# Transposed weights read in contiguous blocks, a narrow split on VectorE, one load queue and a new step order

## The chip, the cores and the metric

The kernel runs on one core of a Trainium2 chip. The metric is the device time of one execution in microseconds (us), the median of repeated runs. The core's engines work side by side: PE (TensorE) multiplies matrices; DVE (VectorE), ACT (ScalarE) and POOL (GpSimd) work on elements; SP (SyncE) issues DMAs here, as ACT can too.

## The reference, cut to what matters

```python
def phi(x):                                  # attention, 4 batches, 4 heads, 1088 tokens, head_dim 32
    a = np.einsum('rd,bhsd->bhsr', S1, x)    # S1, S2: 8 x 32
    b = np.einsum('rd,bhsd->bhsr', S2, x)
    return np.einsum('bhsi,bhsj->bhsij', a, b).reshape(*x.shape[:-1], r * r)
q_p, k_p = (phi(q), phi(k))
kv = np.einsum('bhsf,bhsd->bhfd', k_p, v)
z = np.sum(k_p, axis=2)
num = np.einsum('bhsf,bhfd->bhsd', q_p, kv)
den = np.einsum('bhsf,bhf->bhs', q_p, z)[..., None] + 1e-06
x = num / den                                # then regrouped to 4352 x 128
a = x @ w1                                   # 128 x 1024
b = x @ w2
h = a * b @ w3                               # 1024 x 1024
out = h @ w_out                              # 1024 x 128
```

q, k and v are float32. S1, S2 and the four weights are float64 and arrive as raw 64-bit words.

## The kernel before, in words

**Weights.** The 64-bit words of w1, w2, w_out and w3 come in eleven pieces of 1 MB, `w0` to `w10`: `w0` and `w1` are halves of w1 and w2, `w2` is w_out (called wo), `w3` to `w10` are the eight 128-row blocks of w3. A piece lands in a buffer `raw` (three of them) and is turned into float32 by five steps: `.c` (scaled high words), `.s` (the sign) and `.m` (rounding bits from the low words), three passes on ACT (L337, L345, L349); `.j` on DVE (L360) joins exponent and mantissa; `.a` (L365) adds the sign and rounding words, on POOL for `w3` to `w6` and on DVE for the others. `.load` brings the piece on SP's queue; for w3 it brings two of four 32-row quarters, and `.load2` brings the other two on ACT's queue.

**Fold.** Since the second product follows directly on the first, the kernel computes w3o = w3 @ w_out once. For block ko, step `f{ko}.t` (L392) transposes the block in 32x32 tiles on DVE, `f{ko}.m` (L398) multiplies it with wo in eight steps, and `f{ko}.o` copies the result into w3o.

**Attention.** For each batch b the steps `k{b}.*` load k and v, split k, form the gram matrix of k (`gram`), its pieces `G*`, `T*` and `N*`, the k features `kp` and their product with v (`kv`, `kvr`), from which `kz` or `ky` are made. `kr0` and `kr1` take the last 64 tokens of two batches. `s.*` prepare S1 and S2: `s.words` and `s.pair` turn their words into float32, `s.split` splits each into a leading part and a rest, on POOL, writing every value four times over for the heads, and `s.lead` (ACT) copies the leading part likewise; `s.T` transposes them and `s.P` multiplies them.

**Groups.** The tokens go in eight groups of 512, g = 0 to 7, and a rest of 256, r. The steps `q{g}.*` make the features of the queries (`A0`, `C0`, `sm` and the rest up to `phi`) and multiply them with kz or ky (`x`), up to the group's input `xT`. For group 0 the last steps are `x` and `xt` on PE, `xs` on DVE, `xT` on ACT. Then for each of eight column blocks c of w1 and w2: `g{g}.{c}a` and `g{g}.{c}b` multiply (L1179, L1189), `.c` copies the first product out of PSUM (ACT, L1184), `.m` multiplies the two into `ab` (DVE, L1195), and `g{g}.{c}o` (L1203) adds ab times w3o to the group's output. The output is transposed by `oT` and stored by `st`. PSUM tag "h" has three buffers, shared by a, b, the folds and some small products.

**What sets the order.** `make_steps` returns a dictionary of steps, and the constant `ORDER` names all of them in one list. They are issued in that order, and each engine works on its own instructions in that order: an instruction that waits holds all later ones of its engine. SP's loads have a further rule: with `DEPTH = 4`, a DMA on SP waits until the fourth one before it has landed. The steps `warm0` to `warm9` issue matmuls on zeros (L183) that compute nothing, as many as `WARM` says. `POOL` names the steps that go to GpSimd instead of VectorE.

Of the kernel before, what the change touches and what calls it, by code (L numbers as in the profile page):

```python
# [11 lines left out]
F32 = mybir.dt.float32  # L12
BF16 = mybir.dt.bfloat16
F16 = mybir.dt.float16
I32 = mybir.dt.int32
# [10 lines left out]
WARM = [10, 2, 1, 1, 1, 1, 3, 3, 3, 2]  # L26

BY_PE = ()
QUEUE2 = "act"

DEPTH = 4
# [3 lines left out]
POOL = set("s.split k1.rest k2.rest k1.kp0 k1.kp1 k2.kp0 k2.kp1 w3.a w4.a w5.a w6.a".split())  # L35
# [3 lines left out]
c.zeros k0.zero k0.load0 k0.loadr c.mask k0.load1 s.load c.act s.zero q0.load c.ident w0.load k0.max0 k0.max1  # L39
k0.nat1 w1.load k0.nat0 warm0 k0.tr1 k0.g0 k0.g1 k0.lead0 s.words k0.lead1 k0.l160 k0.rest0 k0.l161 warm1  # L40
k0.gram0 k0.rest1 k0.kT1 s.pair k0.gram1 q0.tr s.split s.lead q0.max w0.c warm2 s.T k0.Gm k0.Gt k0.Ga k0.Gr
q0.l2 k1.zero k1.loadr k1.load kr0.load k0.Gb s.P q0.l1 s.blk s.Pp warm3 k0.ab1 k0.tr0 k0.abc1 w2.load s.blkh
w1.c q0.rm k0.T0 k0.T1 k0.kp1a kh1.load q0.A0 k0.Ta warm4 q0.C0 k0.kT0 k1.max w1.s k0.kp1b k0.Tb w0.m k1.g
q0.sma warm5 k0.N0 k1.lead k0.Ts q1.tr k1.l16 k1.rest warm6 k0.N1 k0.ab0 k0.Na q0.sta kr0.tr k1.gram0 k0.Nb
kr0.kT w1.m q1.max k0.Nh k0.Nl w0.j q0.A1 k0.abc0 k1.gram1 k0.Nf w0.s q0.sha k0.kp0a q0.smy q0.sla kr0.ab k1.kT0
q0.C1 w2.c q0.sca k0.kp0b k1.kT1 q0.C1t q1.l2 q0.sty q0.al q0.shy kr0.abc q1.l1 q0.phi kr0.kp v0.zero v0.load
v0.loadr w3.load kr1.load warm7 k0.kv0 k0.kv1 k0.kv3 k1.gram2 w3.load2 k0.kv2 k2.zero k2.loadr k0.kvr q0.sly
q0.pt0 k0.kvm q0.scy w4.load q0.p01 q0.pt1 q0.pc0 q0.p2 k0.kzt w0.a k1.ab q0.pc1 k2.load k0.kz w4.load2 q0.x
q0.p12 k1.abt w2.m q0.dn k1.Gm q0.de q0.rc w2.s q0.xs w5.load w1.j warm8 q0.xt q1.A0 w2.j q0.xT k1.Gt w5.load2
w1.a warm9 g0.0a w3.c g0.0b q1.sm w2.a g0.1a g0.0c w3.s g0.0m g0.2a k1.Gr g0.1b g0.1c q1.rm g0.2c g0.2b w3.m  # L50
g0.1m w3.j kr1.tr g0.6a w4.c g0.2m w6.load w3.a g0.5a q1.st k2.max g0.6c g0.6b w6.load2 g0.3a k0.kw kr1.kT
q0.restT g0.5c k2.g k2.lead q1.C0 w4.s g0.6m k2.rest f0.t g0.3c g0.5b w4.m k1.Ga q1.sh g0.3b w5.c w7.load w4.j
f0.m k1.Gb q1.load w4.a k2.l16 g0.5m q1.sl w5.m g0.4a g0.3m q1.sca k2.gram0 q1.scy q1.p01 w5.s q1.al k2.gram1
q1.p2 w5.j k2.gram2 f0.o g0.4c q1.p12 k1.T0 k1.T1 w5.a g0.4b f1.t w7.load2 g0.7a w6.c q1.dn k1.Ta g0.0o g0.4m
k1.kp0 w6.m f1.m f2.t w6.s k2.Gm k1.Tb v1.zero v1.loadr w8.load v1.load k3.zero w6.j f2.m g0.7c q1.de q1.restT
f1.o w6.a q2.tr q1.rc q2.max g0.1o f2.o w7.m q1.bs k0.kyt k1.kp1 f3.t g0.2o k3.loadr w8.load2 k3.load g0.7b
q3.tr w10.load w7.c kr1.ab q1.phi f3.m kr1.abc w7.s w9.load w7.j q1.pt1 f3.o w7.a w10.load2 q1.pt0 k1.kv0 q1.pc0
k1.kv3 f4.t k1.kv2 q1.pc1 k1.kv1 k1.kvr g0.3o k0.ky w8.c k2.Gt g0.7m kh2.load f4.m k2.Gr w8.m k1.kw q3.max
k3.max q1.x f4.o g0.4o q1.xT k3.g w8.j w8.s k3.lead g1.1a k1.Ts g1.2a k3.rest q2.l2 g1.1c g1.1b g1.2c w8.a
k3.l16 k1.N0 g1.2b g1.1m w9.load2 k1.N1 g1.4a g1.2m f5.t g1.7a g1.4c w10.c g1.4b k1.Na k1.Nb g1.7b g1.7c k2.Ga  # L60
g1.4m q2.l1 f5.m w10.m w10.j k1.Nl g1.7m w10.s k1.Nh q2.rm k1.kyt g1.0a f5.o g1.5a w10.a w9.c g0.5o k1.ky k2.Gb
w9.s k2.kT1 g1.5b k1.Nf k2.kT0 q2.C0 g1.0c w9.j kh3.load w9.m f7.t k2.ab g1.5c q3.l2 q2.A0 k3.gram0 k2.abt
# [41 lines left out]
def make_steps(ctx, tc, q, k, v, S1, S2, moe_w1, moe_w2, moe_w3, moe_w_out, out):  # L104
# [136 lines left out]
    def _():  # L241
# [7 lines left out]
        for i in range(2):  # L249
            dve.tensor_scalar(t[:, i], hi[:, i], m[:, i:i + 1], m[:, i:i + 1], ALU.add, ALU.subtract)  # L250
# [1041 lines left out]
```

## Time and profile before

| what | us |
|---|---|
| median of 3 runs | 273.92 (271.85 to 274.69) |
| the profiled execution | 269.56 |
| its span, from the first to the last instruction | 267.8 |
| PE busy | 255.1 (95%) |
| VectorE busy | 189.2 (71%) |
| ACT busy | 112.1 (42%) |
| POOL busy | 35.6 (13%) |
| moved by DMA | 22.52 MB, mean 84 GB/s |

The profile is of one execution, so its times are compared with its own span, not with the median. A group of instructions is shown with its source line, the engine, what it writes and reads, shapes, count, busy us and mean ns, and then the engine's idle time before it with what ended it. The rows of digits cut the span into 40 slices of 6.7 us, each digit the busy share in tenths. Matmuls are pipelined: the busy time of PE includes waits inside the pipeline. A float32 matmul shows as two records.

### The profile page before, as it was taken

The page shows a single profiled execution, that of the slowest core. Times are in us where ns is not written, and L with a number is a line of the kernel's source. Part 1 is how long each engine was busy: PE and PEld are TensorE (multiplying, and loading weights), DVE is VectorE, ACT ScalarE, POOL GpSimd, SP SyncE. Part 2 cuts the span into 40 slices and gives each one's busy share as a digit, 9 for nine tenths or more (in the row PEclk, how much of TensorE's full clock was granted, in tenths as well). Part 3 has the DMA queues.
Part 4 walks back from the last instruction along what each step waited for, and adds up shares of the span by engine and source line. Part 5 has one row for each costly group of instructions (what it writes and reads, how often), then busy time and mean ns, then how long its engine had stood idle before and what let it go on. Part 6 is the DMA issues. An engine that isn't in the chain of part 4 may idle for free.

```text
span 267.8 us, 5767 instructions
## 1 busy us (share of the span) xinstructions
PE 255.1 (95%) x2336; PEld 142.0 (53%) x2336; DVE 189.2 (71%) x430; ACT 112.1 (42%) x192; POOL 35.6 (13%) x55
## 2 busy tenths in 40 slices
PE   7789999799898999999999999999999999999994
PEld 2567745476545685444545444444544444444484
DVE  4878899998999999968948959775474645134141
ACT  5486688966689600323322323333113221232220
POOL 3436106675000440000000000000000000000000
PEclk9986999999999999999999999999999999999999
DMA  6888799988970503504100200020020002002020
GB/s 202 281 268 204 159 223 211 230 214 203 219 169 5 163 5 52 157 0 104 21 4 0 40 2 0 2 42 0 2 40 0 2 0 39 0 2 39 0 39 20
DMA packets 31226, 22.52 MB, mean 84 GB/s; under 512 B 21344, under 2 KB 25568, under 8 KB 31072
## 3 DMA queue, kind: packets, MB, share of 16 engines
q1 hardware_dynamic: 28352, 17.44, 27.5%
q10 hardware_dynamic: 2848, 4.72, 7.4%
q8 instruction: 18, 0.29, 0.5%
q14 instruction: 8, 0.07, 0.1%
HBM read 19.93 MB, written 2.23 MB: 83 GB/s over the span
## 4 chain that ended last, share of the span: by engine, by line
PE 69%; DVE 13%; DMA 10%; ACT 4%; issue 1%; POOL 1%; SPq 0%; DVEq 0%; ACTq 0%
PE ps_o L1203 19%; PE b_ps L1189 19%; PE a_ps L1179 19%; DMA raw<-in_moe_w_dram 5%; DVE w3T L392 5%; DMA kk<-in_k_dram 4%; PE ps_xb L1123 3%; PE ps_c L859 2%; PE ps_w3o L398 2%; DVE ab L1195 2%; PE ps_o L1207 1%; DMA s_raw<-in_S_dram 1%; DVE k_g L147 1%; DVE w3c L365 1%; POOL w3c L365 1%
## 5 line engine op out<-in xcount | busy, mean ns | idle before, releaser
L1195 DVE TENSOR_TENSOR ab<-ffa,b_ps 128x512 f32<-128x512 f32 (+1 forms) x72 | 46.6, 650 | 55.7 <-PE b_ps L1189 40.9
L1184 ACT COPY ffa<-a_ps 128x512 f32<-128x512 f32 (+1 forms) x72 | 40.2, 564 | 98.4 <-PE a_ps L1179 89.8
L1189 PE MATMUL b_ps<-xT,w 128*128 128x512 f32 (+1 forms) x144 | 69.2, 574 | 0.0
L1179 PE MATMUL a_ps<-xT,w 128*128 128x512 f32 (+1 forms) x144 | 68.2, 572 | 0.1
L1203 PE MATMUL ps_o<-ab,w3o 128*128 128x512 f32 x128 | 64.3, 600 | 0.0
L1179 PEld LDWEIGHTS a_ps<-xT,w 128*128 128x128 f32 x144 | 26.4, 190 | 29.3 <-issue 23.7
L1189 PEld LDWEIGHTS b_ps<-xT,w 128*128 128x128 f32 x144 | 26.5, 190 | 28.0 <-issue 24.7
L1203 PEld LDWEIGHTS ps_o<-ab,w3o 128*128 128x128 f32 x128 | 23.1, 190 | 25.3 <-issue 21.4
L398 PE MATMUL ps_w3o<-wo,w3T 128*128 128x128 f32 x128 | 15.7, 278 | 3.8 <-DVE ab L1195 2.5
L398 PEld LDWEIGHTS ps_w3o<-wo,w3T 128*128 128x128 f32 x128 | 14.9, 192 | 7.4 <-DVE ab L1195 4.5
L392 DVE STREAM_TRANSPOSE w3T<-w3c 128x1024 f32<-128x1024 f32 x8 | 16.6, 2075 | 0.9 <-POOL w3c L365 0.8
L349 ACT ACTIVATE sg<-raw 128x1024 uint16<-128x1024 uint32 x11 | 15.1, 1377 | 0.8 <-DVE s_pr L1031 0.8
L345 ACT CAST sg<-cv_c 128x1024 f16<-128x1024 f32 x11 | 15.2, 1380 | 0.0
L337 ACT ACTIVATE cv_c<-raw 128x1024 f32<-128x1024 f32 x11 | 12.8, 1161 | 2.7 <-DMA raw<-in_moe_w_dram 1.6
L1137 ACT COPY xT<-ps_xb 128x128 f32<-128x128 f32 (+1 forms) x28 | 5.7, 281 | 16.8 <-PE ps_xb L1123 16.8
L536 POOL TENSOR_TENSOR kp<-kabt 128x1024 f32<-128x1024 f32 x4 | 8.6, 2160 | 27.1 <-DVE kabt L595 27.0
L365 POOL TENSOR_TENSOR w3c<-w3c,sg 128x1024 int32<-128x1024 int32 x4 | 9.6, 2406 | 17.1 <-DVE w3c L360 14.1
L183 PE MATMUL idle_ps<-zeros 128*128 128x512 bf16 x27 | 10.0, 491 | 1.1 <-DVE zeros L158 1.1
L1058 DVE TENSOR_TENSOR ph<-s_al,s_bs 128x1024 f32<-128x1024 f32 (+1 forms) x8 | 9.2, 1144 | 0.1
L836 ACT ACTIVATE q<-qT,q_m 128x512 f32<-128x512 f32 x8 | 5.8, 726 | 6.8 <-DVE s_rc L1045 3.5
L513 PE MATMUL ps_g<-kk 128*32 128x64 f32 x288 | 8.4, 235 | 0.1
L147 DVE TENSOR_REDUCE k_g<-kk 128x1 f32<-128x1152 f32 (+1 forms) x5 | 5.5, 1107 | 4.3 <-DMA kk<-in_k_dram 4.3
(215 smaller groups left out, 312.0 us busy)
## 6 DMA issues: line engine op xcount, KB each, us to landing
raw<-in_moe_w_dram SPq DMA_DIRECT2D x16, 256.0 KB, 5.8
raw<-in_moe_w_dram ACTq DMA_DIRECT2D x16, 256.0 KB, 6.2
qh<-in_q_dram SPq DMA_DIRECT2D x4, 544.0 KB, 4.0
raw<-in_moe_w_dram SPq DMA_DIRECT2D x4, 512.0 KB, 8.0
out_dram<-oT SPq DMA_DIRECT2D x32, 64.0 KB, 2.0
kk<-in_k_dram SPq DMA_DIRECT2D x3, 512.0 KB, 6.8
kh<-in_k_dram SPq DMA_DIRECT2D x12, 128.0 KB, 4.5
v<-in_v_dram SPq DMA_DIRECT2D x12, 128.0 KB, 3.3
```

Source lines behind the costliest of these rows:

```text
L183: pe.matmul(t, zeros[:, :128], bview(zeros, [[0, 2], [1, 256]]), start=True, stop=True)
L337: act.mul(x["c"], words(1).bitcast(F32), 2.0 ** -112)
L345: act.copy(sign, x["c"])
L349: act.mul(bview(sign_bits[n % 2].bitcast(U16), [[2, 1024]]), words(0).bitcast(U32), 2.0 ** -29)
L365: on(f"w{n}.a").tensor_tensor(d, d, sign_bits[n % 2], ALU.add)
L392: dve.transpose(w3T[ko].rearrange("p s (i r) -> p s i r", r=32), bview(w3c[ko], [[1, NC], [256, 4], [NC, 32]]))
L398: pe.matmul(t["o"], w3T[ko][:, c], wo[:, c], start=c == 0, stop=c == NC - 1)
L1179: pe.matmul(x["a"][:, :w], w_of(0, c), xT[g][:, c0:c0 + w], start=True, stop=True)
L1184: act.copy(x["s"][:, :w], x["a"][:, :w])
L1189: pe.matmul(x["b"][:, :w], w_of(1, c), xT[g][:, c0:c0 + w], start=True, stop=True)
L1195: dve.tensor_mul(ab_sb[g, c][:, c0:c0 + w], x["s"][:, :w], x["b"][:, :w])
L1203: pe.matmul(o_ps[g][:, :n], w3o[:, c], ab[:, :n], start=c == 0, stop=c == NC - 1)
```

## The change

1. A w3 block is transposed from contiguous runs of 32 elements: column 32s + r of a quarter, where it was 8r + s. To match, wo is loaded by 32-row quarters too, so that partition p of slice s holds row 256(p // 32) + 32s + p % 32. It gets a `.load2` of its own.
2. `s.split` goes from POOL to DVE and writes each value once; `s.lead` then makes all four parts for the heads in one copy, and `s.P` reads the narrow values.
3. `.load2` goes from ACT's queue to SP's (`QUEUE2`), and `DEPTH` from 4 to 6.
4. `w3.s` and `w5.s` go from ACT to POOL.
5. `ORDER` is new throughout, and so are the places and the number of the idle matmuls: 41 in six places for 27 in ten.

The helper `shape` in the diff leaves every access as it was, since `BY_PE` is empty.

```diff
-WARM = [10, 2, 1, 1, 1, 1, 3, 3, 3, 2]
+WARM = [14, 3, 5, 14, 2, 3]
-QUEUE2 = "act"
+QUEUE2 = "sp"
-DEPTH = 4
+DEPTH = 6
-POOL = set("s.split k1.rest k2.rest k1.kp0 k1.kp1 k2.kp0 k2.kp1 w3.a w4.a w5.a w6.a".split())
+POOL = set("k1.rest k2.rest k1.kp0 k1.kp1 k2.kp0 k2.kp1 w3.a w4.a w5.a w6.a w3.s w5.s".split())
 ORDER = """
-c.zeros k0.zero k0.load0 k0.loadr c.mask k0.load1 s.load c.act s.zero q0.load c.ident w0.load k0.max0 k0.max1
-k0.nat1 w1.load k0.nat0 warm0 k0.tr1 k0.g0 k0.g1 k0.lead0 s.words k0.lead1 k0.l160 k0.rest0 k0.l161 warm1
-k0.gram0 k0.rest1 k0.kT1 s.pair k0.gram1 q0.tr s.split s.lead q0.max w0.c warm2 s.T k0.Gm k0.Gt k0.Ga k0.Gr
-q0.l2 k1.zero k1.loadr k1.load kr0.load k0.Gb s.P q0.l1 s.blk s.Pp warm3 k0.ab1 k0.tr0 k0.abc1 w2.load s.blkh
-w1.c q0.rm k0.T0 k0.T1 k0.kp1a kh1.load q0.A0 k0.Ta warm4 q0.C0 k0.kT0 k1.max w1.s k0.kp1b k0.Tb w0.m k1.g
-q0.sma warm5 k0.N0 k1.lead k0.Ts q1.tr k1.l16 k1.rest warm6 k0.N1 k0.ab0 k0.Na q0.sta kr0.tr k1.gram0 k0.Nb
-kr0.kT w1.m q1.max k0.Nh k0.Nl w0.j q0.A1 k0.abc0 k1.gram1 k0.Nf w0.s q0.sha k0.kp0a q0.smy q0.sla kr0.ab k1.kT0
-q0.C1 w2.c q0.sca k0.kp0b k1.kT1 q0.C1t q1.l2 q0.sty q0.al q0.shy kr0.abc q1.l1 q0.phi kr0.kp v0.zero v0.load
-v0.loadr w3.load kr1.load warm7 k0.kv0 k0.kv1 k0.kv3 k1.gram2 w3.load2 k0.kv2 k2.zero k2.loadr k0.kvr q0.sly
-q0.pt0 k0.kvm q0.scy w4.load q0.p01 q0.pt1 q0.pc0 q0.p2 k0.kzt w0.a k1.ab q0.pc1 k2.load k0.kz w4.load2 q0.x
-q0.p12 k1.abt w2.m q0.dn k1.Gm q0.de q0.rc w2.s q0.xs w5.load w1.j warm8 q0.xt q1.A0 w2.j q0.xT k1.Gt w5.load2
-w1.a warm9 g0.0a w3.c g0.0b q1.sm w2.a g0.1a g0.0c w3.s g0.0m g0.2a k1.Gr g0.1b g0.1c q1.rm g0.2c g0.2b w3.m
-g0.1m w3.j kr1.tr g0.6a w4.c g0.2m w6.load w3.a g0.5a q1.st k2.max g0.6c g0.6b w6.load2 g0.3a k0.kw kr1.kT
-q0.restT g0.5c k2.g k2.lead q1.C0 w4.s g0.6m k2.rest f0.t g0.3c g0.5b w4.m k1.Ga q1.sh g0.3b w5.c w7.load w4.j
-f0.m k1.Gb q1.load w4.a k2.l16 g0.5m q1.sl w5.m g0.4a g0.3m q1.sca k2.gram0 q1.scy q1.p01 w5.s q1.al k2.gram1
-q1.p2 w5.j k2.gram2 f0.o g0.4c q1.p12 k1.T0 k1.T1 w5.a g0.4b f1.t w7.load2 g0.7a w6.c q1.dn k1.Ta g0.0o g0.4m
...
+c.zeros s.zero c.mask k0.zero k0.load0 k0.loadr k0.load1 s.load c.act q0.load v0.zero c.ident kr0.load k0.max0
+w0.load k0.max1 s.words v0.load k0.nat1 k0.g0 s.pair k0.nat0 k0.g1 k0.lead0 k0.lead1 k0.l160 k0.rest0 k0.l161
+warm0 k0.gram0 k0.rest1 s.split k0.gram1 q0.tr s.lead s.P k0.tr0 k1.zero k1.load k0.Gm q0.max k1.loadr s.T
+k0.kT0 q1.tr k0.tr1 kh1.load q0.l2 s.blkh k0.Gt s.blk q0.l1 k0.Ga k0.Gr warm1 k0.ab0 k0.kT1 q0.rm w1.load kr0.tr
+k0.ab1 k0.Gb k0.abc0 s.Pp k0.kp0a k0.abc1 kr0.kT w0.c k0.kp1a v0.loadr q1.max warm2 k0.T0 k0.T1 k0.kv0 w3.load
+q0.A0 k0.Ta k0.kp1b q0.C0 k1.max w3.load2 k0.kp0b k0.Tb kr0.ab q0.sma k0.kv1 k0.Ts k1.g k0.N0 q0.sta k1.lead
+k0.kv2 k0.kv3 k0.N1 q0.sha k1.l16 k1.rest k1.kT0 k0.Na w0.m q0.sla q0.sca k1.kT1 w1.m w2.load k0.Nb k0.Nh k0.Nf
+q0.al warm3 q0.A1 k0.Nl q0.C1 w2.load2 q0.smy kr0.abc w0.s q0.phi kr0.kp k1.gram0 k0.kvr q0.sty q1.l2 warm4
+q0.pt0 k0.kvm q0.shy q0.C1t q0.pt1 q0.sly q0.pc0 w0.j k0.kzt k1.ab q0.pc1 q0.scy k0.kz q0.p01 w1.c q0.x q0.p2
+k1.abt q1.l1 q0.p12 w5.load q0.dn w1.s q0.de q0.rc w5.load2 k1.gram1 q0.xs q1.A0 kr1.load w0.a q0.xt q0.xT w1.j
+w3.c warm5 g0.0a q1.rm g0.0b w2.c w1.a k1.gram2 g0.0c w3.j w3.s g0.3a w3.m k1.Gm k1.Gt q1.sm g0.7a g0.0m g0.3c
+w4.load w3.a g0.3b g0.7c g0.5a w5.c g0.3m q0.restT g0.7b k0.kw g0.5c q1.st w5.s f0.t w5.m g0.5b kr1.tr g0.2a
+q1.sh w2.m w5.j q1.C0 w2.j w5.a w2.s g0.7m q1.sl g0.5m g0.1a g0.2c q1.scy q1.sca g0.1b w2.a g0.1c k2.zero
+k2.loadr w4.load2 w7.load k2.load w7.load2 w6.load g0.2b w4.c g0.1m g0.6a kr1.kT w4.s q1.al w4.j f0.m w6.load2
+q1.p01 w4.m q1.p2 g0.2m q1.p12 g0.4a f2.t g0.6c w4.a q1.load g0.6b g0.4c k2.max f0.o k0.kyt g0.0o k0.ky q1.dn
+w7.c k2.g f2.m q1.de k2.lead g0.6m w7.m k2.rest f1.t g0.4b k2.l16 kr1.ab q1.rc k1.Ga f1.m q1.bs w7.s k1.Gr k1.Gb
...
     @step("s.split")
     def _():
         hi, lo = (x.rearrange("p (i d) -> p i d", i=2) for x in (sk["a"].bitcast(F32), sk["m"]))
-        m, t = sk["g"], sb("sk_t", [r, 2, D])
-        sk["abs"] = x = sb("pT", [r, 3, 2, H, D], name="sk_abs")
-        wide = lambda y: bview(y, [[D, 2], [0, H], [1, D]])
-        dve = on("s.split")
+        m, t = bview(sk["g"], [[1, 2], [0, D]]), sb("sk_t", [r, 2, D])
+        sk["x"] = x = sb("sk_x", [r, 6, D])
+        both = lambda n, by: bview(x[:, n], [[by * D, 2], [1, D]])
         dve.tensor_mul(sk["m"], sk["m"], sk["c"])
-        dve.tensor_scalar(m, m, 2.0 ** 16, None, ALU.mult)
-        for i in range(2):
-            dve.tensor_scalar(t[:, i], hi[:, i], m[:, i:i + 1], m[:, i:i + 1], ALU.add, ALU.subtract)
-        dve.tensor_add(x[:, 2], wide(hi), wide(lo))
-        dve.tensor_sub(hi, hi, t)
-        dve.tensor_add(x[:, 1], wide(hi), wide(lo))
-        sk["t"] = wide(t)
+        shift_in(dve, t, hi, m, 8)
+        shift_out(dve, both(0, 4), t, m, 8)
+        dve.tensor_sub(t, hi, both(0, 4))
+        dve.tensor_add(both(1, 2), hi, lo)
+        dve.tensor_add(both(2, 3), t, lo)
     @step("s.lead")
     def _():
-        act.copy(sk["abs"][:, 0], sk["t"])
+        sk["rep"] = sb("pT", [r, 4, H, D], name="sk_rep")
+        act.copy(sk["rep"], bview(sk["x"], [[D, 4], [0, H], [1, D]]))
...
-            elif n == 2:
-                sp.dma_start(raw[n], moe_w_out.rearrange("(p s) d -> p (s d)", s=NC))
             else:
                 quarter(sp, 0)
-                quarter(sp, 1)
+                quarter(sp, 2)
         def quarter(eng, t):
-            src = bass.AP(tensor=moe_w3.tensor, offset=moe_w3.offset + (n - 3) * 128 * DF + t * 256,
-                          ap=[[DF, 32], [32 * DF, 4], [1, 256]])
+            if n == 2:
+                src = bass.AP(tensor=moe_w_out.tensor, offset=moe_w_out.offset + t * 256 * DM,
+                              ap=[[DM, 32], [32 * DM, NC], [1, DM]])
+            else:
+                src = bass.AP(tensor=moe_w3.tensor, offset=moe_w3.offset + (n - 3) * 128 * DF + t * 256,
+                              ap=[[DF, 32], [32 * DF, 4], [1, 256]])
             eng.dma_start(raw[n][t * 32:(t + 1) * 32], src)
-        if n > 2 and n - 3 not in BY_PE:
+        if n >= 2 and n - 3 not in BY_PE:
             @step(f"w{n}.load2")
             def _():
-                for t in (2, 3):
+                for t in (1, 3):
                     quarter({"pool": pool, "act": act, "sp": sp}[QUEUE2], t)
...
             @step(f"f{ko}.t")
             def _():
                 w3T[ko] = sb("w3T", [128, NC, 128], bufs=2)
-                dve.transpose(w3T[ko].rearrange("p s (i r) -> p s i r", r=32), bview(w3c[ko], [[1, NC], [256, 4], [NC, 32]]))
+                dve.transpose(w3T[ko].rearrange("p s (i r) -> p s i r", r=32), bview(w3c[ko], [[32, NC], [256, 4], [1, 32]]))
```

The two beginnings of `ORDER` reach past the first FFN steps and the first fold; the later part is reordered likewise.

## The prediction, made before the changed kernel was run

> **What bounds the kernel now.** I read the slices of the span first, then the stages, then the chain of waits, then single stretches of the timeline.
>
> ```profile
> PE   7789999799898999999999999999999999999994
> DVE  4878899998999999968948959775474645134141
> PEclk9986999999999999999999999999999999999999
> DMA  6888799988970503504100200020020002002020
> ```
>
> PE is full from about the 15th slice (100 us) on; before that VectorE is as full as PE, and the DMA engines are near full for eleven slices. The same in four stages, cut at the first FFN matmul (`g0.0a`, 35.5) and at the end of `k3.gram2` (98.5); after the times stand busy us of PE, weight loads, DVE, ACT and POOL:
>
> ```profile
> 0.00:35.50 35.50, 30.47 (x449) 21.05 (x449) 26.71 (x80) 23.09 (x34) 13.47 (x41) 0.90 0.80 223
> 35.50:98.50 63.00, 59.03 (x677) 38.45 (x677) 60.42 (x112) 45.43 (x60) 22.10 (x14) 1.00 0.74 167
> 98.50:255.00 156.50, 156.39 (x1158) 74.45 (x1156) 99.07 (x234) 41.47 (x92) 0.00 (x0) 1.00 0.12 24
> ```
>
> PE's busy time counts waits inside the pipeline, so I price PE by the distance from start to start where it runs dense. In the chain, late:
>
> ```profile
> 119.37 0.86 PE a_ps L1179 x2
> ```
>
> An FFN step costs 0.86. So 192 steps make 165.0, the last group 10.4, eight folds of 1.89 make 15.1, and the q, k and S work, priced alike, 47.6: 238.1 us useful, plus 27 idle (warming) matmuls. Before `g0.0a` lie 17.6 us of it, so 220.5 remain, and 267.8 - 35.5 - 220.5 = 11.8 us are lost later: 5.0 in the second stage (58.0 of 63.0 used), 3.4 in small pieces after 98.5, 3.5 behind the last matmul. Only the start of `g0.0a` and those 5.0 us can move.
>
> What causes the 5.0: the view of L398, the folds' matmuls, gives who ended its idle time (us, times):
>
> ```profile
>   DVE ab L1195: 7.0, 5
>   DVE w3T L392: 3.4, 4
> ```
>
> Both enders are VectorE's (60.4 busy of 63). Its dearest item there is the w3 transpose, and the same operation on as many elements, read contiguously, takes 1.23 for 2.08; in the groups:
>
> ```profile
> L392 DVE STREAM_TRANSPOSE w3T<-w3c 128x1024 f32<-128x1024 f32 x8 | 16.6, 2075 | 0.9 <-POOL w3c L365 0.8
> L1069 DVE STREAM_TRANSPOSE pT<-ph 128x1024 f32<-128x1024 f32 x6 | 7.4, 1232 | 0.0
> ```
>
> What sets 35.5: in VectorE's timeline the start of `xs` follows a wait for `ps_kv` and a queue of other work, `w0.a` (L365) among it:
>
> ```profile
> 29.42 0.29 DVE L627 TENSOR_TENSOR kvm<-ps_kv,mask 128x128 f32<-128x128 f32 x1 [0.77 <-PE ps_kv L620]
> 30.37 1.22 DVE L365 CUSTOM_DVE_ANT_0 w<-w,sg 128x2048 uint16<-128x2048 uint16 x1
> 33.45 0.69 DVE L1101 TENSOR_TENSOR xs<-ps_xt,s_rc 128x512 f32<-128x512 f32 x1 [0.25 <-PE ps_xt L1095]
> ```
>
> In PE's timeline, what made `ps_kv` late, and three idle matmuls:
>
> ```profile
> 29.04 0.32 PE L620 MATMUL ps_kv<-kpr,v 128*32 128x64 f32 x8 [0.43 <-POOL v L443]
> 19.29 1.49 PE L183 MATMUL idle_ps<-zeros 128*128 128x512 bf16 x3
> ```
>
> `k0.kvr` waits for a POOL memset standing behind `kr0.kp`, and the phi transposes queue behind it. VectorE has done 25.2 us of work (start to start) when `xs` begins at 33.45; of the other 8.2, half is the wait for the first load, half is scattered waits like the one shown.
>
> [...] the granted clock was 0.50 in 20 to 24 us, and the three idle matmuls above took 0.43 each, against 0.21 warm. [...]
>
> **The change, part by part.**
>
> *Transposes.* The durations give 2.075 - 1.232 = 0.84, so 8 x 0.84 = 6.7 us off VectorE, all between 45 and 95 us. Bounds: 0, if the stride is not the cause, and 6.7; I take 6.7. It is worth only what PE waits for, at most the 5.0.
>
> *wo in 32-row quarters.* Four DMAs of 1 KB pieces for one of 8 KB pieces; k's loads have 1 KB pieces too, 512 KB in 6.8 us beside others. It is needed only by `f0.m` (45 us); nothing on the path.
>
> *S split.* POOL took 3.4 (8.53 to 11.94). Six small DVE operations at about 0.2 (the `s.pair` rows) are 1.2 on the full engine; `s.lead` grows from 0.40 to 0.59 (512 elements, ffa's row). Net VectorE: -6.7 + 1.2 = -5.5.
>
> *Signs w3.s, w5.s.* ACT loses 2 x 1.24. POOL has no such row: lower bound 1.1 (its 512-element product), upper 2.4 (L365); [...] I take 2.0. `w3.a` then waits on `w3.m` anyway (35.3), so both bounds cost nothing; if ACT did `w3.m` earlier, up to 2.4 on `f0.t`.
>
> *Queues.* 16 issues leave ACT (0.3 to 0.5 each, mostly under running operations: ACT idled only 0.35 us for issue), so I book nothing; at most 16 x 0.4 = 6.4 of ACT's time where ACT is late. SP gets 19 more, 119 in all at about 0.5: 60 us, and it has gaps. Six loads in flight for four. `k1.load` still waits for the grams (one kk buffer), about 10.6 for 12.1, and lands by 16; `k1.max`, which waited 1.15 us for it, is now due at 17.5. `w1.load`, issued at 5.2 before, now stands behind it: about 14.5, and is due at 22.8 (`w1.m`).
>
> *Waits added.* On ACT `k1.l16` waits for `k1.lead` (16.7 to 20.5), and behind it stands `w0.m`, which frees the buffer that `w2.load` needs on SP: 22.8; wo is due at 44. Behind `w2.load` stand `w5.load` (free after `w1.c`, 28.6; due 36) and `kr1.load` (due 39). `w4.load` waits for `w3.m` (35.3), `w7.load` for `w2.m` (40.3), and behind it stands `k2.load`: issued 41.5, and at 6.8 (kk's row) landed 48.3. If it is late, `k2.max` holds all of VectorE.
>
> *Idle matmuls.* 41 for 27: 14 more, 3.0 us at 0.21, 6.0 at 0.43. Fourteen cover the first loads; fourteen (`warm3`) stand in front of `q0.A1`, where VectorE's `k0.Nh` is due at 23.5 anyway: nothing if warm (20.6 + 3.0 = 23.6), up to 3 if cold. I take warm, since PE is busier there than before.
>
> *New order, walked by hand on all queues with these rows.* S words 5.5, `k0.rest1` 8.4, S split 9.6, grams 10.5 (10.0 before), `s.T` 12.1, `s.blk` 12.8, `k0.T1` 16.8 (15.0: five idle matmuls and `s.Pp` ahead), `k0.N1` 20.6 (21.0), `warm3` to 23.6, `k0.Nh` 23.5, `q0.smy` 24.0, phi 24.3 to 25.4 (28.4 before: `w0.j`, `q1.max` and `k1.kT` no longer stand between). `v0.zero` is early, so `kvr` ends 25.3; transposes 26.7; ACT copies and kz 27.5; `q0.x` 29.7; `xs` 30.4 (`w0.a` now behind it); `xT` 31.5; `g0.0a` 31.7. VectorE would be idle about 1 us in all after the first load, against about 4 before; [...] I take 32.7. 17.0 us useful precede it, so 221.1 remain.
>
> Then PE, walked to `f3.m` with three "h" buffers, never waits: f0 at 44.9, f2 49.7, f1 52.8, f4 59.2, f3 69.8. VectorE needs 49 us where PE needs 56 to `k3.gram2`, so the stage turns from VectorE's to PE's. Near misses: `k2.load` lands 48.3, `k2.max` is due 48.2; w4 and w7 land within 1 us of need. For them and jitter I leave 1.7 of the 5.0. The late 6.9 stay: 99.1 of 156.5 busy leaves VectorE slack there.
>
> Sum: 32.7 + 221.1 + 1.7 + 6.9 = 262.4, that is 5.4 under 267.8. The profiled execution took 269.56 (span + 1.8); the median, 273.92, lies 4.4 higher. I take the difference off the median: 268.5.
>
> **Rivals.**
>
> *The walk literally (265.8).* `g0.0a` at 31.7 and no loss in the second stage: 2.7 more gained. For: the walk. Against: the kernel before loses such pieces too.
>
> *Half the gain (272).* `warm3` runs cold: 14 x 0.43 = 6.0, or 4.7 if the clock returns midway, so `q0.A1` is 2 us late; and the folds wait for jitter as before (3.3 of 5.0 lost): 268.5 + 2.0 + 1.6 = 272.1. For: 0.50 at exactly that place. The change not doing what it says ends here too: if contiguous runs did not help the transpose, VectorE stays full, the 5.0 stay, and 271.8 results.
>
> *Slower: the single load queue (278).* From 35.3 (w3's buffer free) to w10, SP must bring 9.1 MB (six w3 blocks of 1.05, k2, q1, k3, v1, kh2). At 220 GB/s, about what full slices show, w10 lands at 76.7; `f7.m` is due about 86 and the conversion takes 6.5, so 79.5 is free. Each later us delays PE by one. At 170 GB/s it lands at 88.8: +9.3, 277.8. It decides against the change below 174 GB/s (landing 87.6). For: buffer waits block everything behind them, and 58 to 62 us, half idle, gives 138. Against: six in flight, and stages of 4 us between 30 and 58 show 191 to 265.
>
> **How the numbers follow.** Likeliest 0.46 (own range 266.5 to 270.5), literal walk 0.14, half 0.26, slower 0.14. About 1% (2.7 us) is what measurement tells apart. Faster: 0.46 + 0.14 + 0.08 of "half" = 0.68; same: 0.18 + 0.02 = 0.20; slower 0.12. The range reaches over the literal walk and "half" to 264.5 and 274.5; most of the slower case is left out.
>
> **What would show it.** Right: L392's successor near 1.23; `g0.0a` between 32 and 34; idle before the fold's matmuls below 3; phi ending by 27. Wrong: clock 0.5 around 20 to 25 with `warm3` over 4; `k2.max` or `w10`'s conversion waiting for DMA; `g0.0a` later than 34.5; PE idle for VectorE after 98 us.

## The result and the profile after

| | before | after |
|---|---|---|
| median of the runs side by side (four each), us | 272.88 (270.83 to 274.69) | 262.07 (261.84 to 262.68) |
| ratio | | 0.9609, 95% interval 0.9531 to 0.9688 |
| profiled execution, us | 269.56 | 261.84 |
| its span, us | 267.8 | 260.1 |
| its mean granted clock | 0.987 | 1.0 |
| first FFN matmul (`g0.0a`), us | 35.5 | 32.2 |
| end of the last fold's matmuls, us | 96.6 | 91.9 |

The kernel is faster by 3.9%. The forecast was 268.5, range 264.5 to 274.5: the sign is right, the size is 6.4 us short. Here and below, medians are of all runs, while ratios leave out those over 1.5% above the fastest of the same kernel.

The slices of the kernel after, in the same form as those of before:

```profile
PE   6899999999999999999999999999999999999994
DVE  3889979999999999879338958955889623232331
PEclk9999999999999999999999999999999999999999
DMA  6879979969899010260002002000200002020020
```

PE is now full from the third slice on instead of the 15th. The clock never falls. VectorE is still full in the middle, but PE no longer waits for it. The stages, cut at `g0.0a` and at the end of the last gram (columns as before):

```profile
0.00:32.23 32.23, 28.78 (x427) 19.85 (x427) 25.60 (x82) 19.83 (x32) 9.99 (x33) 1.00 0.88 232
32.23:88.67 56.44, 56.44 (x619) 36.22 (x620) 53.55 (x107) 45.93 (x61) 24.82 (x15) 1.00 0.86 204
```

In the second, PE is busy for the whole 56.44 us, and VectorE has 53.55 us of work: the stage has turned from VectorE's to PE's, as forecast. The transposes' group, from the page:

```profile
L396 DVE STREAM_TRANSPOSE w3T<-w3c 128x1024 f32<-128x1024 f32 x8 | 9.9, 1234 | 0.1
```

And who ended the idle time in the view of the folds' line (us, times), where before had 7.0 and 3.4:

```profile
  DVE w3T L396: 0.7, 2
  DVE ab L1199: 0.3, 1
```

This view adds the waits of the weight loads to those of the matmuls. The loads run ahead and overlap: those of the first fold start at 45.77, its matmuls at 46.16, and in the second stage 36.22 us of loads lie beside 56.44 us of matmuls within 56.44 us. So the view's sums are not time lost. The matmuls alone, before and after:

```profile
L398 PE MATMUL ps_w3o<-wo,w3T 128*128 128x128 f32 x128 | 15.7, 278 | 3.8 <-DVE ab L1195 2.5 <-DVE w3T L392 1.2
L402 PE MATMUL ps_w3o<-wo,w3T 128*128 128x128 f32 x128 | 15.6, 275 | 0.0
```

Before, they waited 3.7 us for VectorE; after, not at all.

In the head, by which I mean all that lies ahead of `g0.0a`, from VectorE's timeline, `w0.a` stands behind `xs` now, and the wait for `ps_kv` is gone:

```profile
25.69 0.29 DVE L631 TENSOR_TENSOR kvm<-ps_kv,mask 128x128 f32<-128x128 f32 x1
...
30.16 0.69 DVE L1105 TENSOR_TENSOR xs<-ps_xt,s_rc 128x512 f32<-128x512 f32 x1
30.76 1.22 DVE L369 CUSTOM_DVE_ANT_0 w<-w,sg 128x2048 uint16<-128x2048 uint16 x1
```

From PE's timeline, `warm3` and `k0.kvr`:

```profile
20.80 3.19 PE L182 MATMUL idle_ps<-zeros 128*128 128x512 bf16 x14
25.30 0.32 PE L624 MATMUL ps_kv<-kpr,v 128*32 128x64 f32 x8 [0.22 <-POOL kpr L688]
```

The fourteen idle matmuls took 3.19 us (0.22 us from start to start) at a granted clock of 1.0, so they ran warm; the three of before, at 0.50, took 0.43 each.

### The profile page after: what moved, and what is told of

Read it like the earlier page. It is cut to its first block, busy times and chain, and to the rows that moved or that the text cites. A ratio compares the mean times of both kernels' runs of the same rounds, so it can differ in the third digit from the quotient of the medians.

```text
span 260.1 us, 5778 instructions
## 1 busy us (share of the span) xinstructions
PE 253.1 (97%) x2350; PEld 141.1 (54%) x2350; DVE 185.6 (71%) x436; ACT 109.4 (42%) x190; POOL 36.6 (14%) x50
## 4 chain that ended last, share of the span: by engine, by line
PE 89%; DMA 7%; SPq 2%; ACT 1%; issue 0%; POOL 0%; ACTq 0%
PE b_ps L1193 23%; PE a_ps L1183 23%; PE ps_o L1207 22%; PE ps_w3o L402 6%; DMA raw<-in_moe_w_dram 5%; PE ps_c L863 3%; PE ps_xb L1127 3%; DMA kk<-in_k_dram 2%; PE ps_g L517 2%; PE ps_o L1211 1%; PE ps_ab L592 1%; PE ps_kv L617 1%; PE ps_xt L1099 1%; PE ps_ph L1080 1%; ACT sg L353 1%; PE ps_a L863 0%
## 5 line engine op out<-in xcount | busy, mean ns | idle before, releaser
L1199 DVE TENSOR_TENSOR ab<-ffa,b_ps 128x512 f32<-128x512 f32 (+1 forms) x72 | 46.7, 654 | 49.1 <-PE b_ps L1193 34.2
L1193 PE MATMUL b_ps<-xT,w 128*128 128x512 f32 (+1 forms) x144 | 67.8, 574 | 0.0
L1183 PEld LDWEIGHTS a_ps<-xT,w 128*128 128x128 f32 x144 | 26.3, 190 | 29.2 <-issue 25.4
L1220 DVE STREAM_TRANSPOSE oT<-ps_o 128x512 f32<-128x512 f32 x8 | 5.7, 716 | 10.3 <-PE ps_o L1207 10.3
L540 POOL TENSOR_TENSOR kp<-kabt 128x1024 f32<-128x1024 f32 x4 | 9.7, 2430 | 18.9 <-DVE kabt L599 18.9
L182 PE MATMUL idle_ps<-zeros 128*128 128x512 bf16 x41 | 11.2, 419 | 1.1 <-DVE zeros L157 1.1
L349 ACT CAST sg<-cv_c 128x1024 f16<-128x1024 f32 x9 | 12.2, 1360 | 0.0
L396 DVE STREAM_TRANSPOSE w3T<-w3c 128x1024 f32<-128x1024 f32 x8 | 9.9, 1234 | 0.1
L517 PE MATMUL ps_g<-kl 128*32 128x32 bf16 x144 | 6.9, 180 | 1.8 <-ACT kl L505 1.8
L1073 DVE STREAM_TRANSPOSE pT<-ph 128x1024 f32<-128x1024 f32 (+1 forms) x7 | 8.1, 1155 | 0.1
```

Source lines behind the costliest of these rows:

```text
L182: pe.matmul(t, zeros[:, :128], bview(zeros, [[0, 2], [1, 256]]), start=True, stop=True)
L349: act.copy(sign, x["c"])
L396: dve.transpose(w3T[ko].rearrange("p s (i r) -> p s i r", r=32), bview(w3c[ko], [[32, NC], [256, 4], [1, 32]]))
L517: pe.matmul(o[h * D:(h + 1) * D], lhs, rhs, start=start, stop=stop, skip_group_check=True)
L1183: pe.matmul(x["a"][:, :w], w_of(0, c), xT[g][:, c0:c0 + w], start=True, stop=True)
L1193: pe.matmul(x["b"][:, :w], w_of(1, c), xT[g][:, c0:c0 + w], start=True, stop=True)
```

## The experiments

Each was timed beside the kernel before, in five groups (e1 to e4, e5 to e8, e9 to e12, e13 to e16, e17 and e18). Together these hold 118 runs of the kernel before: median 271.3, from 267.8 to 275.8. Its medians by group are 270.8 to 271.8, so differences of under 1 us between groups say nothing. All kernels at a glance (clock: lowest and highest of the runs; the last two columns are from the profiled run; fold times compare only within one order):

| kernel | median | ratio to before | clock | `g0.0a` | folds' end |
|---|---|---|---|---|---|
| e1_strided | 267.38 | 0.9903 (0.9875 to 0.9930) | 0.994 to 1.0 | 32.4 | 97.2 |
| e2_b_contig | 268.57 | 0.9940 (0.9912 to 0.9967) | 0.966 to 0.992 | 38.2 | 96.7 |
| e3_order | 282.60 | 1.0458 (1.0393 to 1.0523) | 0.974 to 0.982 | 37.6 | 113.3 |
| e4_parts | 266.81 | 0.9889 (0.9834 to 0.9944) | 0.968 to 0.986 | 35.1 | 94.0 |
| e5_two_queues | 277.27 | 1.0215 (1.0137 to 1.0293) | 0.969 to 0.980 | 36.1 | 106.3 |
| e6_few_idle | 267.95 | 0.9896 (0.9827 to 0.9964) | 0.960 to 0.974 | 36.8 | 97.2 |
| e7_b_idle | 269.43 | 0.9916 (0.9884 to 0.9947) | 0.985 to 1.0 | 33.8 | 94.9 |
| e8_split_signs | 266.13 | 0.9827 (0.9757 to 0.9896) | 0.987 to 1.0 | 33.3 | 95.8 |
| e9_depth4 | 265.42 | 0.9788 (0.9724 to 0.9851) | 0.994 to 1.0 | 33.5 | 95.2 |
| e10_act_six | 279.58 | 1.0221 (1.0123 to 1.0319) | 0.969 to 0.981 | 34.2 | 106.2 |
| e11_signs | 263.41 | 0.9714 (0.9659 to 0.9769) | 0.997 to 1.0 | 32.7 | 94.1 |
| e12_parts_idle | 266.46 | 0.9825 (0.9766 to 0.9885) | 0.987 to 1.0 | 34.1 | 93.0 |
| e13_no_warm3 | 264.78 | 0.9751 (0.9696 to 0.9805) | 0.985 to 0.987 | 34.0 | 93.8 |
| e14_b_one_queue | 271.13 | 0.9949 (0.9915 to 0.9982) | 0.966 to 0.994 | 36.5 | 98.0 |
| e15_later | 265.62 | 0.9775 (0.9727 to 0.9822) | 0.997 to 1.0 | 31.8 | 95.0 |
| e16_b_idle2 | 268.92 | 0.9909 (0.9873 to 0.9945) | 0.993 to 1.0 | 36.0 | 97.1 |
| e17_b_v_early | 272.08 | 1.0060 (1.0028 to 1.0092) | 0.979 to 1.0 | 38.1 | 99.5 |
| e18_parts_v_early | 266.94 | 0.9837 (0.9799 to 0.9876) | 0.987 to 1.0 | 35.9 | 94.8 |

### The transposes, in the new order and in the old

e1_strided, from the kernel after:

```diff
-dve.transpose(..., bview(w3c[ko], [[32, NC], [256, 4], [1, 32]]))
+dve.transpose(..., bview(w3c[ko], [[1, NC], [256, 4], [NC, 32]]))     # and wo in one load, as before
```

> The changed kernel with only the transposes put back: w3T reads every eighth word again and wo comes in one load. Theory A (my steps: the contiguous read takes 6.7 us off VectorE in the middle stage, and PE waits there for VectorE): the changed kernel has 53.6 us of VectorE work in the 56.4 us of that stage, so 6.7 more make 60.3 and PE waits at least 3.9 us: 266 us. Theory D (the new order carries the gain and hides the transposes): 263.5 or less. Theory C (a VectorE that is full in the middle turns small delays into waits, and so makes the times of the kernel before spread over 4 us): the times spread over more than 2.5 us; by theories A and B (the head's clock) they stay within 1.5.

Measured 267.38, that is 5.3 more than after. The head is as after (32.4); the folds end 5.3 later. In the view of the folds' line VectorE's transposes, at 2.06 us each again, are back as the ender (again with the weight loads; 2.1 us for the matmuls alone):

```profile
  DVE w3T L398: 5.3, 4
```

From `g0.0a` to the folds' end PE is idle for 3.6 of 64.8 us, where it was never idle after. Theory A holds, theory D falls. The spread is 1.8 us, between the bounds of theory C (over 2.5) and of A and B (1.5), so by itself it decides little; the next run does.

e2_b_contig, from the kernel before (the same line turned the other way, wo in four loads):

> The kernel before with only the contiguous transposes (wo in four loads on the same queue). Theory A: at most the 5.0 us of the middle stage: 268 to 269.5, against 272.9. Theory C: the spread closes to under 1.5 us, and with it the median falls further, to 265 or 266. Theory B (the variable loss is the half clock in the head, where PE idles): the spread stays near 4 us. Theory D: under 1.5 us of gain.

268.57, with the transposes at 1.24 us each: some 2.2 less than before in its group (1.6 by the ratio), and still spread over 4.0 us at clocks down to 0.966: with the transposes cheap the spread stays, so theory C falls. From `g0.0a` to the end of the grams it takes 60.2 us for 63.0: 2.8 of the 5.0 come back, though `g0.0a` comes 2.7 later in this profiled run (clock 0.968), which may help that stage. What idle time remains in the view of the folds' line is ended by `ab` on VectorE (5.4 us), not by a transpose.

### The order alone, and the parts alone

e3_order: the new `ORDER` and `WARM`, all else of before.

> The new order and its idle matmuls alone, all else as before (strided transposes, wide split on GpSimd, second load queue on ScalarE, four loads in flight, signs on ScalarE). Theory B: the clock in the head stays 1.0 as in the changed kernel, the start of the first FFN step moves from 35.5 to about 33, the spread falls under 1.5 us: 266 to 268, the rest being VectorE's 6.7 in the middle. Theory Q (the second load queue on ScalarE, with four in flight, makes the variable loss): the spread stays near 4 us, median 269 or more.

282.60, slower than before by 4.6%. Neither theory had that. GpSimd waited 23.8 us for the words of w3's blocks, and ScalarE, which makes them, 11.4 for loads of raw words. e4_parts: the opposite, everything but `ORDER` and `WARM`.

> All parts of the change without the new order: the old order and the old idle matmuls (the new second load of wo stands right after the first). Theory B: the head stays as it was, clock 0.5 about 20 to 24 us, spread near 4 us, gain only the transposes', 268 to 269.5. Theory Q: the spread falls under 1.5 us and the median to 266. Theory D: under 1.5 us of gain, or a loss, since the order was not made for these costs.

266.81, between theories B and Q, at clocks of 0.968 to 0.986. So the parts alone give 4.0 in their group (3.0 by the ratio), the order alone loses 11.8, and both together gain about 9 on the 118 runs. The effects do not add; the next runs say why.

### What the new order needs: the queue, the depth, the split and the signs

e5_two_queues and e9_depth4, from the kernel after, with e10_act_six between them:

```diff
-QUEUE2 = "sp"
-DEPTH = 6
+QUEUE2 = "act"      # e5 and e10; e9 keeps "sp"
+DEPTH = 4           # e5 and e9; e10 keeps 6
```

> The changed kernel with only the loads put back: the second half of each weight load on ScalarE's queue, four in flight. The new order alone took 282.6, since the conversion of w3's blocks waited for loads (GpSimd waited 23.8 us for the signs, ScalarE 8.6 for the raw words). Theory Q (the new order needs the single queue and the six in flight): most of that loss comes back: 270 to 278. Theory S (the split and the signs are what the order needs): within 2 us of the changed kernel, 262 to 264. My step, which booked the queues at nothing (at most 6.4 of ScalarE's time): 262 to 268.

> The changed kernel with four loads in flight instead of six, still on the single queue. Theory Q1 (it is the depth: with four in flight the queue moves too few bytes where the new order needs them, 150 to 165 GB/s in the slices from 27 to 41 us of the two-queue run against 211 to 253): most of the 15 us come back, 270 to 277. Theory Q2 (it is ScalarE's queue: its loads stand behind work that waits, so half a block comes late): 262 to 265.

> The changed kernel with the second half of each weight load on ScalarE's queue, but six in flight on the other. Theory Q2: 270 to 277, with ScalarE and GpSimd waiting for the raw words of w3's blocks. Theory Q1: 262 to 265.

277.27, 265.42 and 279.58. The depth alone is worth 3.4 us. With ScalarE's queue the runs spread, from 276.2 to 281.5 (e5) and from 276.1 to 282.1 (e10): the queue costs at least 14 us, and the two depths can't be told apart there. Theory Q2 holds, with a part for Q1, and my "nothing" for the queues fails in this order. ScalarE's timeline of e10 shows how (ACTq is ScalarE's issue of a DMA):

```profile
45.81 0.59 ACT L1188 COPY ffa<-a_ps 128x512 f32<-128x512 f32 x1 [0.61 <-PE a_ps L1183]
45.82 1.77 ACTq L322 DMA_DIRECT2D raw<-in_moe_w_dram  x4
53.22 1.11 ACT L341 ACTIVATE cv_c<-raw 128x1024 f32<-128x1024 f32 x1 [6.82 <-DMA raw<-in_moe_w_dram]
```

The second half of `w4` is issued at 45.8, once ScalarE has come through copies that wait for PE, and the conversion starts at 53.22. In the kernel after SP issues it by 38.8 and the same instruction runs at 44.26:

```profile
44.26 1.17 ACT L341 ACTIVATE cv_c<-raw 128x1024 f32<-128x1024 f32 x1
```

Nine us late at `w4`, and the folds follow: their last matmul ends at 106.2 for 91.9. Part of that is the clock: the mean granted clock of e10's profiled run is 0.981, that of the kernel after 1.0. Here a second issuing engine costs the wait for the instructions ahead of the load on that engine (issued at 45.8 for 38.8). In the old order ScalarE waits at most 0.7 us for any load from 20 to 100 us, so there is little for the same edit to gain. e14_b_one_queue (the kernel before with `"sp"` and 6):

> The kernel before with all loads on the sync queue and six in flight, nothing else. All parts without the new order took 266.8, the transposes alone 268.6, the kernel before 270.9. My step (queues booked at nothing): 270 to 272. If the queues carry the other 1.8 us of the parts: 268.5 to 269.5, with ScalarE's issue time (16 x 0.4 us) gone from its path. If the old order needs ScalarE's queue as the new one needs the single one: over 274.

271.13 against 271.82 in its group: next to nothing, as my step said, for that order.

e8_split_signs (the wide split on GpSimd and the signs on ScalarE, both as before) and e11_signs (the signs alone), from the kernel after:

```diff
-POOL = set("k1.rest ... w6.a w3.s w5.s".split())
+POOL = set("k1.rest ... w6.a".split())      # e11; e8 has "s.split" in it and the old s.split, s.lead, s.T and s.P too
```

> The changed kernel with the wide split on GpSimd and all signs on ScalarE, as before; contiguous transposes, single queue and the new order stay. By my walk the split ends at 12.0 instead of 9.6, the transposes of S with it, and the first FFN step comes at most 2 us later; the signs cost nothing as long as ScalarE has gaps: 262 to 264. Theory S (the new order needs these two parts): 268 or more. If ScalarE is late by w3.s and w5.s (2.5 us): 264 to 266, with the first folds later.

> The changed kernel with the signs of w3 and w5 on ScalarE; the split stays narrow on VectorE. Both put back took 266.1, with the first FFN step at 33.3 against 32.2 and the folds' end 3.8 later. By my step (the split is worth 1.0 to 2 us of the head, the signs nothing while ScalarE has gaps): 262 to 262.8. If ScalarE is late and w3.m and what follows it slip by 2 x 1.24 us: 264 to 265, with the first fold near 48 instead of 46.2, and the head as in the changed kernel.

263.41 for the signs: 1.3, between my two forecasts, with the first fold at 47.6 instead of 46.2. So ScalarE is late there, which I had named as the other bound ("up to 2.4 on `f0.t`") and not taken. On GpSimd they took 1.72 and 1.37 us for my 2.0, an estimate between the two bounds. 266.13 for both, so the split is worth 2.7 in this order by the medians; in the profiled runs it is 1.7, of which 0.6 have arisen by `g0.0a` and the rest by the folds' end.

### The clock

The 118 runs of before lie along a line against the granted clock (correlation -0.73):

| granted clock | runs | median, us |
|---|---|---|
| 0.985 and more | 12 | 268.9 |
| 0.971 to 0.985 | 64 | 270.6 |
| under 0.971 | 42 | 272.0 |

A straight line through them meets full clock at 267.5 (an estimate, since no run got above 0.994), and 0.01 of clock is 1.4 us. The profiled run, at 0.987, would belong to the few in the first row. Is the clock the cause? e6_few_idle takes idle matmuls away from the kernel after, e13_no_warm3 only `warm3`:

```diff
-WARM = [14, 3, 5, 14, 2, 3]
+WARM = [14, 0, 0, 0, 0, 0]      # e6;  e13: [14, 3, 5, 0, 2, 3]
```

> The changed kernel with the first 14 idle matmuls only, the 27 others left out. Theory B (idle matmuls in the head's gaps hold the array's clock, and that is what the kernel before lacks): the granted clock falls from 1.0 to between 0.96 and 0.99 in most runs, the times spread over 2 us or more, median 264 to 268. Rival (PE has no long gap in the new order, so the idle matmuls are for nothing): 261 to 262.5, spread under 1.5 us.

> The changed kernel without warm3, the 14 idle matmuls ahead of q0.A1. My step: they cost nothing, since VectorE's k0.Nh is due then anyway; the other side of it, that they are worth something, I had not booked. Theory B (without them PE idles 2.8 us, 21.0 to 23.8, and the clock is halved for what follows): clock 0.97 to 0.99, 263.5 to 266. Rival (the earlier idle matmuls suffice): 261.5 to 262.5 at a clock of 0.995 or more.

267.95 (5.9 more) and 264.78 (2.7 more). The stages of e6 from 13 us on (the last three columns are clock, DMA share and GB/s):

```profile
13.00:20.00 7.00, 4.96 (x51) 4.46 (x51) 5.96 (x17) 3.17 (x7) 4.19 (x4) 0.82 0.74 197
20.00:27.00 7.00, 4.94 (x63) 4.23 (x62) 4.13 (x16) 3.77 (x5) 2.68 (x2) 0.50 1.00 255
27.00:32.00 5.00, 4.31 (x81) 3.76 (x85) 4.56 (x15) 2.75 (x4) 0.59 (x1) 0.59 0.87 200
```

PE idles two of every seven us, the clock is halved from about 17.5 us to 31 (by the shares), and `g0.0a` comes 4.6 later. Idle matmuls that my sum had at nothing (or as a cost) carry 5.9 us. The other way round, e7_b_idle puts ten more into the gaps of the kernel before:

```diff
-WARM = [10, 2, 1, 1, 1, 1, 3, 3, 3, 2]
+WARM = [10, 2, 1, 1, 1, 6, 3, 3, 3, 2]      # and 5 in s.T, behind its first transpose
```

> The kernel before with ten more idle matmuls in the two gaps of PE that come ahead of its half clock: five between the first and the second transpose of S (11.0 to 12.0 us in its trace) and five more ahead of k0.N0 (17.6 to 18.8). All else as it was. Theory B: the clock stays above 0.99 in all runs, the spread falls from 6 us to under 2, the median from 270.8 to about 268 (its own fastest runs, at clock 0.994, took 268.0 to 268.5). Rival (the low clock goes along with a loss that has another cause, such as late loads): the clock rises, but the median stays at 270 or more and the spread at 3 or more.

The median falls only to 269.43 and the spread stays at 5.2, which theory B did not have: 5 of the 20 runs still drop to 0.985 or 0.987, at 272 to 273. The nine at 0.997 and above have a median of 268.05. e16_b_idle2 (four more, ahead of `k0.kv0`):

> The kernel before with the ten idle matmuls of the earlier run and four more ahead of k0.kv0, where PE then waited 0.83 us for v. Theory B: the clock holds at 0.99 or above in nearly all runs and with it the time at 267.5 to 268.5, spread under 2 us: then 2.5 to 3.3 us of the 270.9 are half clock. Rival: median 269 or more, spread over 3 us, at a clock of 0.99 or above.

Clock 0.993 and above in all six runs, spread 1.7 against 5.7 for before in its group, median 268.92 against 271.82: 2.9 us and most of the spread go with the half clock. The profiled run, the slowest of the six, shows another loss that the clock does not explain:

```profile
28.23 0.88 PE L617 MATMUL ps_kv<-kp,v 128*32 128x64 f32 x48 [2.99 <-DMA v<-in_v_dram]
```

### What the new order brings beyond the clock

e12_parts_idle, the old order with all parts and eight more idle matmuls in two gaps:

> The old order with all parts of the change (266.8), and eight more idle matmuls in the two gaps of PE ahead of its half clock: two ahead of the transposes of S, six ahead of k0.N0. Theory B (half clock and parts explain most of the gain): the clock stays above 0.99, 263 to 264.5, spread under 2.5 us; then the new order is worth at most 2 us beyond the clock it keeps. Rival (the new order carries more than the clock): 265.5 or more at a clock of 0.99 or above.

266.46 at clocks of 0.987 to 1.0 (265.7 in the profiled run at 1.0). The rival holds: about 4 us of the new order are not the clock. Beside e4, whose clock is lower, the gain is 0.4 by the medians and 1.3 when each is set against before in its own group; the line would give 2, so it does not carry over exactly. Of the 3.8 by which PE ends later than in the kernel after, 1.9 have arisen by `g0.0a`. Is it v, issued at 21 in the old order and at 5.3 in the new?

```diff
-... q0.phi kr0.kp v0.zero v0.load v0.loadr w3.load
+... k0.abc1 v0.zero v0.load v0.loadr w2.load      # e17 from e7_b_idle, e18 from e12_parts_idle
```

> The kernel before with the ten idle matmuls of the earlier run, and batch 0's v (its memset and its two loads) moved in the order from after q0.phi to ahead of wo's load, so that it is issued at about 15 instead of 21 us. With the idle matmuls alone the full-clock runs took 267.8 to 270, and the traces of two such runs show PE waiting 0.83 and 2.99 us for v. Theory V (in the old order v's late load is the second variable loss): no wait of PE for v, 266 to 267.5 at full clock, spread under 2 us. Rival (the loads only trade places, and what now stands behind v is late): 268 or more, with a DMA wait elsewhere in the head.

> The old order with all parts of the change and eight more idle matmuls (266.5), and batch 0's v moved as in the run beside it. Theory V: 264 to 265.5 at full clock, so that of the 4.4 us that the new order brought at full clock 1 to 2.5 are v's load. Rival: 266 or more.

272.08 and 266.94: no gain, the first even a loss. PE no longer waits for v; now VectorE waits 2.6 and 3.4 us for `kh`, which stands behind v. The loads trade places, so theory V falls for this place: v is issued at 14 to 15 here, and no run has it in the old order at 5.3.

e15_later looked for a better version, by moving 2.1 us of VectorE's work out of the head of the kernel after:

```diff
-... k1.rest k1.kT0 ... k1.kT1 w1.m ... k1.ab ... k1.abt q1.l1 ...
+... w5.s f0.t k1.kT0 k1.kT1 k1.ab k1.abt w5.m ...      # and warm3 of 8
```

> The changed kernel with four steps of batch 1 taken out of the head, to after the first fold's transpose (k1.kT0, k1.kT1, k1.ab, k1.abt: 2.1 us of VectorE and 1.1 of PE), and six idle matmuls fewer in warm3. If VectorE bounds the head of the changed kernel (it idles 0.7 us between 16 and 30): the first FFN step comes 0.8 to 1.5 us earlier, at about 31 (ScalarE's w1.s is next), and the middle stage absorbs the 2.1 (53.6 of 56.4 used): 260.5 to 261.5. If the middle stage has no room: 262 to 264. If the clock falls: 264 or more.

265.62, later than any forecast at full clock: `g0.0a` comes only 0.4 earlier, and the middle pays. PE waits there for what was moved:

```profile
40.59 1.56 PE L592 MATMUL ps_ab<-kT,RS 128*32 128x256 f32 x16 [1.76 <-DVE kT L585]
```

No version beat the kernel after. Why the head did not move is in the chain of the kernel after, back from `g0.0a`:

```profile
10.62 0.02 POOL kk L426
10.64 5.75 DMA kk<-in_k_dram
...
16.80 6.24 DMA raw<-in_moe_w_dram
...
23.13 1.36 ACT sg L353
24.49 0.06 ACT krab L682
24.55 0.07 issue
24.62 0.64 POOL kpr L688
```

`k1.zero` and `k1.load` start once the grams have ended (10.49), `w1.load` stands behind them and lands at 23.04, and ScalarE's conversion of it (`w1.m`, at 23.13) holds `kr0.abc`, `kpr` and so `k0.kvr`. But a second path arrives at almost the same time: ScalarE waits 3.48 us for VectorE's `k1.lead`, starts `k1.l16` at 20.59 and ends `w0.m` at 23.02, so without the load `w1.m` would start only 0.1 earlier. In e15 the chain runs over this second path:

```profile
19.62 0.80 DVE kk L499
20.45 1.15 ACT kl L505
21.60 1.23 ACT sg L353
...
22.87 1.38 ACT sg L353
```

L499 is `k1.lead`, the two `sg` are `w0.m` and `w1.m`. The work that e15 moved stands behind `k1.lead` on VectorE, so it could not shorten this path. Loads and VectorE bound the head together, and no run moves both.

## Why the prediction was right and wrong, point by point

**The failed step is the last of the sum: "I take the difference off the median: 268.5".** The span forecast was 262.4 and is 260.1, so 2.3 of the 6.4 us are the sum's. The other 4.1 are the distance of 4.4 between the profiled run of before and the median, which I carried over to the kernel after; there it is 0.2. What that distance was, the runs show in part. 2.6 of it are a high draw of three: the 118 runs have 271.3, and only 8 of them reach 273.9; why these three were so slow stays open, since their clocks are not on record. The other 1.8 go with the clock: the profiled run stood at 0.987, 100 of the 118 at 0.975 and below. The kernel after loses nothing to the clock, so nothing of this distance carries over. By the line, before at full clock takes 267.5, and from there to 262.07 are 5.4 us, the amount that my sum gave; that they agree is luck, since the sum fell 2.3 short and started from a run that by the line held 1.8 of half clock. That the clock causes the loss is shown in the kernel after (e6, e13); for before it rests on the correlation and on e7 and e16, whose runs at 0.997 and above have medians of 268.1 and 268.6.

**Idle matmuls ("nothing if warm")** — they ran warm, right (that a busier PE would keep them so was my estimate; the trace of before did not show it), but I asked only what they cost. In this kernel they keep the clock: without `warm3` it is 0.985 to 0.987 and 2.7 us are lost, without five of the six sets 0.960 to 0.974 and 5.9. The row of 0.50 at 20 to 24 us was read as a danger for the change instead of a loss of the kernel before that the change could take away.

**Transposes** — 1.234 as forecast. In the new order 5.3 are lost when they are put back, in the old 1.6 to 2.2 are gained; "at most the 5.0" was right for the old one. The 7.0 and 3.4 that I took as PE's idle time held the weight loads' too; the matmuls waited 2.5 and 1.2.

**The middle loss (1.7) and the late 6.9** — together 8.6. Behind `g0.0a` 260.1 - 32.2 - 221.1 = 6.8 were lost, so the 1.7 left for jitter did not come, which is most of the sum's 2.3: the folds' matmuls wait for nothing.

**The walk of the head** — `g0.0a` 32.2 for 32.7 (the 1.0 of it above the walk's 31.7 was an estimate of mine), `warm3` to 24.0 for 23.6, phi 24.3 to 25.5 for 24.3 to 25.4, `xs` 30.2 for 30.4, f0 46.2 for 44.9, f3 70.5 for 69.8. Close, but with half of the bound: I had VectorE, whose `k1.lead` does hold ScalarE to 20.6 as I had it (20.5); the chain shows the load beside it, since `w1.load`, for which I had about 14.5, was issued at 16.4 and landed 0.1 late.

**Signs and queues (nothing)** — for the signs the other bound holds (1.3 in the new order). For the queues, nothing is right in the old order (e14); the new order depends on them (3.4 for the depth, at least 14 for the queue). So no term was missing from the sum, but the reason given ("ACT idled only 0.35 us for issue") was beside the point.

**The rivals** — the slower one, a single load queue that brings w10 too late, is refuted: the slices from 39 to 85 us show 211 to 256 GB/s but for one of 140, and `w10.c` starts at 82.0 without waiting for a load. It was close, though: the last part of w10, issued at 73.6 and 6.2 on the way, landed about 79.8, where I had called up to 79.5 free. In this order two queues were the greater danger. "Half the gain" fell on both of its legs. The "literal walk" (265.8) was nearest, and its span was right: 31.7 + 221.1 + 6.9 = 259.7 for 260.1, with no loss in the second stage, as it had it. It missed by the same last step.

**Open**: which moves of the new order bring the 4 us at full clock beyond the parts. The clock is excluded by e12; v's load, moved by itself to 14 or 15 us, brought nothing (e17, e18).

## What to carry to other kernels

Before taking a forecast difference off a median, ask what sets the distance between the profiled run and the median: whether the median is of enough runs, and, if the clock row shows a dip, how much of the median is that dip. Here idle matmuls in PE's gaps alone took the dip and 2.9 us off the kernel before (e16), so a change that fills such gaps may gain that on top of its own. Price idle matmuls by what follows when they are gone (2.7 us for `warm3`), not by their length (3.19). In e10 a load on a computing engine's queue was issued only when that engine's program came to it (45.8 us for 37.7), so an order of steps and a choice of queues are one edit; here the order alone lost 12 us.

## What the hardware showed that was not expected

The granted clock fell after short gaps of PE: in the kernel before PE idled 1.0 us at 11 to 12 and 1.2 at 17.6 to 18.8, and the clock was 0.50 from about 18.5 to 25; in e13 one gap of 2.5 us, ended at 23.5, left 0.71 in 20 to 24, 0.50 in 24 to 28 and 0.93 in 28 to 32. The length of a gap does not decide alone: in e16's profiled run PE stood idle for 2.99 us, up to 28.23, longer than in any of these, and the clock stayed full:

```profile
PEclk9999999999999999999999999999999999999999
```

What else decides, no run here shows. Which run of one and the same kernel falls, and how far, differs: mean clocks of 0.956 to 0.994 over the 118 runs of before.
